# A fused attention and mixture-of-experts kernel: the tile scheduling layer replaced by a recorder with its own semaphores

## Chip, cores, metric

One Trainium2 chip, one NeuronCore. The metric is the device time of one execution in microseconds; the kernel before has a median of 174.42 us over three runs (174.42 to 174.47). Five engines matter: TensorE (PE, its weight loads PEld), VectorE (DVE), ScalarE (ACT), GpSimd (POOL) and SyncE (SP), which here only issues DMAs and waits. Sixteen DMA engines carry all data between memory and SBUF.

## What is computed

Linear attention over 8 batches of 8 heads (576 positions, 64 columns a head), a normalization of each row, and a soft mixture of 8 experts with 4 slots each over all 4608 tokens. All arithmetic is in float32.

```python
kv = np.einsum('bhsd,bhse->bhde', k, v)
out = np.einsum('bhsd,bhde->bhse', q, kv)
x = out / np.sqrt(np.mean(out * out, axis=-1, keepdims=True) + 1e-06) * g_norm   # -> (4608, 512)
logits = x @ phi                                   # 32 slots
d = softmax(logits, over tokens);  slot_input = d.T @ x
slot_out[e] = np.maximum(slot_input[e] @ w1[e], 0.0) @ w2[e]
result = softmax(logits, over slots) @ slot_out
```

## The kernel before, in words

The 4608 tokens are 36 tiles of 128. For each batch the kernel builds the 64x64 products of k and v (class `Kv`, products at L195, L210), places them with phi in a block-diagonal matrix `bd`, and for each token tile multiplies q with it (`products`, L254 and L263), squares, evicts and normalizes. Tiles go in 19 stages of two or one, and six groups of six tiles, each with a running maximum and a partial sum over tokens. After the last group come eight experts (`expert_h` L638, `expert_y` L656), then the mixing of their outputs back to the tokens: `output`, called for two column halves, three token chunks and two parts each, twelve times in all, with products at L701, evictions on ACT (L712) and DVE (L714, the split ones L709 and L710).

All inputs live in one SBUF arena of 160 KB a partition, whose places are written out by hand in tables (`KV_AT`, `Q_AT`, `W_AT`, `OUT_AT`): a place is loaded, read, then overwritten by a later load or by the staged output. Every DMA is issued from SP: `load_row` (L85) and the first load (L123) bring k, v and q; `load_w` (L114) brings the expert weights in eight rows; L718 stores the output in four pieces. There are 24 DMAs. The order of the work is that of the program text: the context manager at L777 takes `manual_schedule`, so the layer orders nothing. What it does is three things. It gives the tiles of each pool (`const`, `wk`, `psA`, `psB`) an address, buffers of a tag taking turns. It works out from the addresses which instruction has to wait for which, and puts semaphore waits and increments on the instructions; for DMAs it has eight semaphores that take turns, and a DMA waits for the one that held its semaphore before. At the end (all its instructions carry L777) SP waits for the DMAs, all engines meet in a barrier, POOL clears the range of semaphores, and all meet again. An earlier barrier at the start belongs to the program's constructor (L769).

The two pools of PSUM have these banks: `psA` two buffers of two banks for `o`, two banks for `kv`, one each for `m` and `s`; `psB` two banks for `y` and three buffers of two banks for `m`.

```python
    const = ctx.enter_context(tc.tile_pool(name="const", bufs=1))
    wk = ctx.enter_context(tc.tile_pool(name="wk", bufs=2))
    ...
    ps = psA.enter_context(tc.tile_pool(name="psA", bufs=1, space=bass.MemoryType.PSUM))
    ...
    ps = ctx.enter_context(tc.tile_pool(name="psB", bufs=3, space=bass.MemoryType.PSUM, reuse_waits="tile"))
```

Of the kernel before, what the change touches and what calls it, by code (L numbers as in the profile page):

```python
# [1 line left out]

# [5 lines left out]

F32 = mybir.dt.float32
BF16 = mybir.dt.bfloat16  # L10
# [4 lines left out]
P = 128  # L15
# [39 lines left out]
SHARED = (5, 11)  # L55
HEAD = 144
SCRATCH = 1024
EPS_RMS = 1e-6
EPS_SUM = 1e-9


def row_length(row):
    return sum(UNIT if part is None else UNIT // 2 for _, _, part in row)


@with_exitstack
def soft_moe_linear_attention(ctx: ExitStack, tc: tile.TileContext, first_in, kv_in, q0_in, q1_in, kv4_in, kv5_in, t3_in, w_in, out):


    nc = tc.nc  # L70

    const = ctx.enter_context(tc.tile_pool(name="const", bufs=1))
    wk = ctx.enter_context(tc.tile_pool(name="wk", bufs=2))
    arena = const.tile([P, HEAD + ARENA], F32, name="arena")
    phi_sb = arena[:, :128].rearrange("p (g w n) -> p g w n", g=2, w=2)
    g2 = arena[:, 128:129]
# [71 lines left out]
    eps = const.tile([P, 1], F32, name="eps")  # L148
    nc.gpsimd.memset(eps, EPS_RMS)
    sel32 = const.tile([P, NS], F32, name="sel32")  # L150
# [20 lines left out]
    run_max = [const.tile([P, 1], F32, name=f"rmax{i}") for i in range(2)]  # L171
    acc = const.tile([P, 129], F32, name="acc")

    psA = ExitStack()
    ps = psA.enter_context(tc.tile_pool(name="psA", bufs=1, space=bass.MemoryType.PSUM))


    class Kv:
# [10 lines left out]
        def products(self, r):  # L189
            g, w = divmod(r, 2)  # L190
            main = kv_main(self.b, g).rearrange("p (r w c n) -> p r w c n", r=2, w=2, c=4)
            for c in range(4):
                for i in range(2):
                    lo = 64 * i
                    nc.tensor.matmul(  # L195
                        self.pkv[lo : lo + 64, w, g],
                        lhsT=main[:, w, 1, c, lo : lo + 64],
                        rhs=main[:, w, 0, c, lo : lo + 64],
                        start=c == 0 and (g == 0 or self.b == 0),
                        stop=False,  # L200
                    )
# [96 lines left out]
    def newton(s):  # L298
        n, ms, r0 = STAGES[s], mss.pop(s), r0s.pop(s)
        r = wk.tile([P, n, H], F32, tag="r", name=f"r{s}", bufs=3)  # L300
        t = wk.tile([P, n * H], F32, tag="r1", name=f"r1{s}")
        nc.vector.scalar_tensor_tensor(out=t, in0=ms, scalar=EPS_RMS, in1=r0, op0=ALU.add, op1=ALU.mult)
        nc.vector.scalar_tensor_tensor(out=t, in0=t, scalar=-0.5, in1=r0, op0=ALU.mult, op1=ALU.mult)
# [120 lines left out]
    first = {b: 9 * (b // 2) + 4 * (b % 2) for b in range(B)}  # L424
# [53 lines left out]
    for g in range(2):  # L478
        kv = Kv(0, "o" if g else "kv", 2 if g else None)
# [10 lines left out]
    for T in range(NT - 2):  # L490
# [3 lines left out]
        o = products(T)  # L494
        s = ends.get(T - 1)
# [36 lines left out]
    s, G = len(STAGES) - 1, len(GROUPS) - 1  # L532
# [51 lines left out]
    last = NE - 1  # L584
# [10 lines left out]
    rs = const.tile([P, 1], F32, name="rs")  # L595
    nc.vector.tensor_scalar_add(rs, acc[:, 128:129], EPS_SUM)
    nc.vector.reciprocal(rs, rs)
    psA.close()


    ps = ctx.enter_context(tc.tile_pool(name="psB", bufs=3, space=bass.MemoryType.PSUM, reuse_waits="tile"))
    W = 2 * GROUPS[0] + 1

    def combine(k):
# [7 lines left out]
        nc.vector.tensor_reduce(out=cs, in_=C, axis=AX.X, op=ALU.add)  # L612
        nc.vector.tensor_scalar_add(cs, cs, EPS_SUM)
        nc.vector.reciprocal(cs, cs)
# [151 lines left out]
def build_program():  # L766
    import concourse.bacc as bacc

    nc = bacc.Bacc("TRN2", target_bir_lowering=False, num_devices=1, dynamic_dma_scratch_size=SCRATCH)  # L769
    shapes = {  # L770
        "first": (P, HEAD + 2304), "kv": (4, P, TOK), "q0": (P, TOK), "q1": (P, 2048),
        "kv4": (P, 2560 + TOK), "kv5": (P, 2 * TOK), "t3": (P, 3 * TOK),
        "w": (1, 2 * NE * P * UNIT),
    }
    args = [nc.dram_tensor(f"in_{n}_dram", s, F32, kind="ExternalInput").ap() for n, s in shapes.items()]
    args.append(nc.dram_tensor("out_0_dram", (1, 4 * NCH * P * 4 * CT * NS), F32, kind="ExternalOutput").ap())
    with tile.TileContext(nc, schedule_with_timeline_sim=True) as tc, tc.manual_schedule():  # L777
        soft_moe_linear_attention(tc, *args)
    return nc


# [56 lines left out]
```

## Time and profile before

| what | value |
|---|---|
| median of 3 runs | 174.42 us (174.42 to 174.47) |
| profiled execution, first to last instruction (its span) | 172.9 us |
| median less span | 1.5 us |
| instructions | 4638 |
| busy: PE, PEld, DVE, ACT, POOL | 150.1, 109.0, 86.3, 89.0, 57.2 us |
| bytes read and written | 61.94 MB and 9.44 MB |
| granted TensorE clock, mean | 0.976 |

The profiled execution has no time of its own beside its span; what the runs' time holds beyond the span is not in the profile. Times in the rows are from the span's start. "PEld" are weight loads, which overlap products. A "q" behind an engine's name means its sequencer: it waits, issues a DMA or handles semaphores, and is not counted as busy. The granted clock is 1.00 in every stretch with products and falls to 0.50 only after the last of them.

### The profile page before, as it was taken

To read this page: it belongs to the slowest core of one execution; us is meant where nothing else is said; L and a number is where in the kernel's file an instruction comes from. 1 tells how busy PE (TensorE), PEld (TensorE's weight loads), DVE (VectorE), ACT (ScalarE), POOL (GpSimd) and SP (SyncE) were. 2 spreads that over 40 slices of the span, in tenths; PEclk is the share of its full clock that TensorE was granted. 3 is DMA by queue.
4 is the path that set the end of the run, shared out by engine and by line. 5 is a ranking of instruction groups with operands and counts; after the bars stand their busy time and mean duration, and the time that the engine had idled before them with its cause. 6 is when DMAs were issued, how large, how long until landed. Compare 5 with 4: busy or idle time off the path is not lost.

```text
span 172.9 us, 4638 instructions
## 1 busy us (share of the span) xinstructions
PE 150.1 (87%) x1975; PEld 109.0 (63%) x1975; DVE 86.3 (50%) x184; ACT 89.0 (51%) x230; POOL 57.2 (33%) x68
## 2 busy tenths in 40 slices
PE   7888897989999899999899989889999989989300
PEld 3457777889688888898796766346665544545000
DVE  1122156383677364763926897625887036228300
ACT  2036486787966888668759863203223035227400
POOL 6000708548356665456582489100000000000000
PEclk9999999999999999999999999999999999999955
DMA  5999999999999998999999998999999999999994
GB/s 188 417 429 426 446 403 449 438 424 471 413 409 443 479 461 359 394 453 402 451 468 428 426 425 368 426 445 400 459 419 428 425 425 403 443 392 401 453 392 199
DMA packets 3476, 71.67 MB, mean 414 GB/s; under 512 B 384, under 2 KB 384, under 8 KB 384
## 3 DMA queue, kind: packets, MB, share of 16 engines
q1 hardware_dynamic: 3456, 71.38, 97.0%
q8 instruction: 15, 0.25, 0.6%
q14 instruction: 5, 0.04, 0.1%
HBM read 61.94 MB, written 9.44 MB: 413 GB/s over the span
## 4 chain that ended last, share of the span: by engine, by line
PE 50%; DMA 23%; ACT 10%; DVE 6%; issue 3%; SPq 2%; DVEq 0%
PE o L263 16%; DMA arena<-in_kv_dram 13%; DMA arena<-in_w_dram 10%; PE kvp_kv L195 8%; PE po L701 5%; PE pY L656 5%; PE pS L412 4%; PE ph L638 2%; PE fill L467 2%; ACT sq L273 2%; PE o L254 2%; ACT arena L712 2%; ACT bd L230 1%; ACT xall L281 1%; SPq L85 1%
## 5 line engine op out<-in xcount | busy, mean ns | idle before, releaser
L263 PE MATMUL o<-bd,arena 128*128 128x192 f32 x256 | 49.3, 336 | 1.7 <-ACT bd L240 1.1
L263 PEld LDWEIGHTS o<-bd,arena 128*128 128x128 f32 x256 | 40.8, 190 | 5.0 <-ACT bd L240 1.6
L286 DVE TENSOR_REDUCE ms<-sq 128x16 f32<-128x1024 f32 (+1 forms) x19 | 22.1, 1162 | 32.2 <-ACT sq L273 32.0
L313 POOL TENSOR_TENSOR xall<-xall,r 128x512 f32<-128x512 f32 x34 | 34.8, 1046 | 0.0
L335 POOL TENSOR_TENSOR part<-part,r 128x512 f32<-128x512 f32 x17 | 17.8, 1050 | 50.4 <-DVE r L304 44.9
L273 ACT ACTIVATE sq<-o 128x512 f32<-128x512 f32 x36 | 21.5, 598 | 11.9 <-PE o L263 11.6
L281 ACT COPY xall<-o 128x512 f32<-128x512 f32 x34 | 20.6, 606 | 0.0
L195 PE MATMUL kvp_kv<-arena 128*64 128x64 f32 x480 | 17.3, 225 | 2.6 <-DMA arena<-in_kv_dram 1.9
L195 PEld LDWEIGHTS kvp_kv<-arena 128*64 128x64 f32 x480 | 15.2, 138 | 6.5 <-DMA arena<-in_kv_dram 2.8
L348 DVE TENSOR_REDUCE logits<-part 128x64 f32<-128x512 f32 (+1 forms) x18 | 17.8, 992 | 0.0
L656 PE MATMUL pY<-arena,xall 128*32 128x256 f32 x256 | 15.0, 380 | 0.2 <-DMA arena<-in_w_dram 0.2
L701 PE MATMUL po<-logits,z 32*128 32x384 f32 x96 | 12.8, 521 | 1.5 <-ACT arena L712 0.9
L638 PE MATMUL ph<-arena,sTe 128*32 128x256 f32 x224 | 12.7, 379 | 0.3 <-DVE sTe L585 0.3
L712 ACT COPY arena<-po 128x768 f32<-128x768 f32 x12 | 9.1, 801 | 7.4 <-PE po L701 7.4
L714 DVE COPY arena<-po 128x768 f32<-128x768 f32 x10 | 9.3, 955 | 7.0 <-PE po L701 7.0
L656 PEld LDWEIGHTS pY<-arena,xall 128*32 128x32 f32 x256 | 8.4, 110 | 6.7 <-issue 1.6
L280 ACT COPY part<-o 128x256 f32<-128x256 f32 x34 | 12.6, 370 | 0.0
L412 PE MATMUL pS<-xall,d 128*32 128x129 f32 x288 | 10.8, 277 | 1.2 <-ACT d L400 1.1
L701 PEld LDWEIGHTS po<-logits,z 32*128 32x128 f32 x96 | 6.1, 183 | 7.1 <-ACT arena L712 4.2
L638 PEld LDWEIGHTS ph<-arena,sTe 128*32 128x32 f32 x224 | 7.2, 110 | 5.3 <-DVE sTe L585 0.7
L412 PEld LDWEIGHTS pS<-xall,d 128*32 128x32 f32 x288 | 7.2, 109 | 4.4 <-issue 3.5
L294 ACT ACTIVATE r<-ms,eps 128x16 f32<-128x16 f32 x17 | 5.2, 308 | 5.9 <-DVE ms L286 5.9
(99 smaller groups left out, 148.3 us busy)
## 6 DMA issues: line engine op xcount, KB each, us to landing
arena<-in_w_dram SPq DMA_DIRECT2D x4, 4096.0 KB, 19.8
arena<-in_w_dram SPq DMA_DIRECT2D x1, 7168.0 KB, 27.6
arena<-in_t_dram SPq DMA_DIRECT2D x1, 6912.0 KB, 36.4
arena<-in_w_dram SPq DMA_DIRECT2D x1, 5120.0 KB, 17.8
arena<-in_kv_dram SPq DMA_DIRECT2D x2, 2304.0 KB, 23.6
arena<-in_kv_dram SPq DMA_DIRECT2D x1, 4608.0 KB, 43.1
out_dram<-arena SPq DMA_DIRECT2D x2, 2304.0 KB, 9.5
arena<-in_kv_dram SPq DMA_DIRECT2D x1, 3584.0 KB, 32.3
```

The source lines that it names most:

```text
L195: nc.tensor.matmul(self.pkv[lo : lo + 64, w, g], lhsT=main[:, w, 1, c, lo : lo + 64], rhs=main[:, w, 0, c, lo : lo + 64], start=c == 0 and ...
L263: nc.tensor.matmul(o[:, r, :192], lhsT=q_main(2 * g + i)[:, r, at : at + P], rhs=bds[i][:, r], start=True, stop=True)
L273: nc.scalar.activation(sqs[s][:, T - starts[s]], o[:, :, 32:160], AF.Square, scale=0.125)
L281: nc.scalar.copy(xts[T % NX][:, :, :128], o[:, :, 32:160])
L286: nc.vector.tensor_reduce(out=mss[s], in_=sqs.pop(s).rearrange("p t j (w d) -> p (t j w) d", w=2), axis=AX.X, op=ALU.add)
L313: nc.gpsimd.tensor_tensor(out=x, in0=x, in1=r[:, i].rearrange("p (j w) -> p j w", w=2).unsqueeze(3).to_broadcast([P, 4, 2, D]), op=ALU.mult,)
L335: engine.tensor_tensor(out=part, in0=part, in1=rs_of[s].unsqueeze(3).to_broadcast([P, STAGES[s], H, NS]), op=ALU.mult)
L348: nc.vector.tensor_reduce(out=L[:, pos(starts[s]) : pos(starts[s]) + STAGES[s]], in_=parts.pop(s).rearrange("p t h n -> p t n h"), axis=AX ...
L412: nc.tensor.matmul(pS[32 * j : 32 * j + 32], lhsT=ds[G][:, i], rhs=x[:, j], start=i == 0, stop=i == GROUPS[G] - 1)
L638: nc.tensor.matmul(ph[32 * j : 32 * j + 32], lhsT=sTe[:, (4 * e + c) * NS : (4 * e + c + 1) * NS], rhs=w_block("w1", e, 4 * c + j), start= ...
L656: nc.tensor.matmul(pY[32 * j : 32 * j + 32, hf, :256], lhsT=hTs[e][:, c], rhs=w_block("w2", u, at + c), start=e == 0 and c < 4, stop=e == ...
L701: nc.tensor.matmul(po[:, 0 if apart else u, : CT * NS].rearrange("p (g x) -> p g x", g=2), lhsT=z[f][lo : lo + 32], rhs=cT[k][lo : lo + 32 ...
```

## The change

The layer goes, and with it its context managers. In its place the kernel file has its own small classes. `Order` stands where the program object stood: each call on an engine (`nc.vector...`) is written down with its operands, `add` works out what it has to wait for, `settle` drops what is already known, and `emit` issues all of it in the same order with semaphores.

```diff
+WORK = {
+    "kvT": (1, 256), "sq": (2, 1024), "part": (3, 512), "ms": (3, 16), "r0": (2, 16), "r": (3, 16), "r1": (2, 16),
+    "top": (1, 128), "diag": (1, 32), "d": (2, 192), "alpha": (2, 1), "cm": (2, 13), "cs": (2, 13),
+}
...
+    def add(self, engine, method, args, kwargs):
...
+        for ap in reads:
+            m = self.memories.get(ap.tensor.name)
+            if m is not None:
+                rows, cols = m.cells(ap)
+                for w in np.unique(m.writer[rows, cols]):
+                    if w >= 0 and (self.ops[w].engine != engine or self.ops[w].dma or engine != "tensor"):
+                        deps.add(int(w))
+                if m.bank:
+                    self.others(deps, m, rows, cols, engine)
+        m = self.memories.get(out.tensor.name) if out is not None else None
+        if m is not None:
+            rows, cols = m.cells(out)
+            for w in np.unique(m.writer[rows, cols]):
+                if w >= 0 and (self.ops[w].engine != engine or self.ops[w].dma):
+                    deps.add(int(w))
+            self.others(deps, m, rows, cols, engine)
...
+    def settle(self, op, deps):
+        known = self.known[op.engine]
+        for d in sorted(deps, reverse=True):
+            w = self.ops[d]
+            key = ("dma", d) if w.dma else w.engine
+            if known.get(key, -1) >= d:
+                continue
+            op.waits.append(w)
+            w.signals = True
+            known[key] = d
+            for k, v in w.known.items():
+                if known.get(k, -1) < v:
+                    known[k] = v
+        op.known = dict(known)
+
+    def emit(self):
+        nc = self.nc
+        counters = {e: nc.alloc_semaphore(f"done_{e}") for e in ENGINES[:4]}
...
+            *before, last = sorted(op.waits, key=lambda w: w.i) or [None]
+            for w in before:
+                engine.wait_ge(w.sem, w.value)
+            inst = getattr(engine, method)(*args, **kwargs)
+            if last is not None:
+                inst.wait_op(last.sem, last.value, "sem-ge")
+            if op.dma:
+                op.sem, op.value = nc.alloc_semaphore(f"dma_{op.i}"), 16
+                sems.append(op.sem)
+                inst.then_inc(op.sem, 16)
+            elif op.signals:
+                counts[op.engine] += 1
+                op.sem, op.value = counters[op.engine], counts[op.engine]
+                inst.then_inc(op.sem, 1)
+        for op in self.ops:
+            if op.dma and not op.signals:
+                nc.sync.wait_ge(op.sem, 16)
+        numbers = sorted(s.num for s in sems)
+        assert numbers == list(range(numbers[0], numbers[-1] + 1))
+        nc.sync.sem_clear(range(numbers[0], numbers[-1] + 1))
...
-    const = ctx.enter_context(tc.tile_pool(name="const", bufs=1))
-    wk = ctx.enter_context(tc.tile_pool(name="wk", bufs=2))
+    const = Const(nc)
+    wk = Pool({tag: [nc.sbuf([P, n], F32, f"{tag}{i}") for i in range(bufs)] for tag, (bufs, n) in WORK.items()})
+    banks = nc.psum(8)
...
-    ps = psA.enter_context(tc.tile_pool(name="psA", bufs=1, space=bass.MemoryType.PSUM))
+    ps = pool(o=(2, 0, 2), kv=(2, 4), m=(1, 6), s=(1, 7))
...
-    ps = ctx.enter_context(tc.tile_pool(name="psB", bufs=3, space=bass.MemoryType.PSUM, reuse_waits="tile"))
+    ps = pool(y=(2, 0), m=(2, 2, 4, 6))
...
-    with tile.TileContext(nc, schedule_with_timeline_sim=True) as tc, tc.manual_schedule():
-        soft_moe_linear_attention(tc, *args)
+    order = Order(nc)
+    soft_moe_linear_attention(order, *args)
+    order.emit()
```

`Memory` keeps for each tensor the last writer and the last reader of every cell: four groups of 32 partitions by single columns in SBUF, by banks of 512 columns in PSUM. In PSUM a reader also waits for readers of the same bank on other engines (`others`). `Pool.tile` gives the buffers of a tag in turn. A DMA has a semaphore of its own. Only an operation that someone waits for increments its engine's semaphore. At the end SP waits for those DMAs that nobody waited for (the four stores) and clears the range of semaphores; the other engines stop after their last instruction. The body of the kernel, its order and its loads and stores are the same text.

## Rows read from the trace of the kernel before

**Rows 1.** The page: the span, and busy time by engine.
```profile
span 172.9 us, 4638 instructions
...
PE 150.1 (87%) x1975; PEld 109.0 (63%) x1975; DVE 86.3 (50%) x184; ACT 89.0 (51%) x230; POOL 57.2 (33%) x68
```

**Rows 2.** The page: busy tenths of the DMA engines in 40 slices; packets, MB, share.
```profile
DMA  5999999999999998999999998999999999999994
...
q8 instruction: 15, 0.25, 0.6%
```

**Rows 3.** Busy by stretch: us, busy (count) by engine; last clock, DMA share, GB/s.
```profile
0.00:1.70 1.70, 0.65 (x2) 0.28 (x3) 0.53 (x2) 0.97 (x1) 0.89 (x8) 1.00 0.00 0
...
20.00:68.00 48.00, 45.27 (x602) 39.44 (x603) 27.34 (x56) 36.17 (x100) 26.73 (x27) 1.00 1.01 432
...
71.00:104.00 33.00, 31.28 (x404) 26.57 (x406) 21.87 (x47) 24.84 (x71) 19.25 (x19) 1.00 1.02 435
...
151.90:153.40 1.50, 1.50 (x29) 0.94 (x32) 0.46 (x1) 0.48 (x1) 0.00 (x0) 1.00 0.78 332
```

**Rows 4.** Timeline of SP: DMA issues, their start and duration in us.
```profile
0.74 0.38 SPq L123 DMA_DIRECT2D arena<-in_first_dram  x1
...
1.64 0.42 SPq L85 DMA_DIRECT2D arena<-in_q_dram  x1
2.11 0.65 SPq L85 DMA_DIRECT2D arena<-in_kv_dram  x1
...
145.43 0.35 SPq L718 DMA_DIRECT2D out_dram<-arena  x1
...
152.53 0.34 SPq L718 DMA_DIRECT2D out_dram<-arena  x1
...
158.18 0.33 SPq L718 DMA_DIRECT2D out_dram<-arena  x1
...
162.28 0.33 SPq L718 DMA_DIRECT2D out_dram<-arena  x1
```

**Rows 5.** The same issues in order: KB each, us from issue to landing.
```profile
arena<-in_q_dram SPq DMA_DIRECT2D x1, 1024.0 KB, 9.9
...
arena<-in_kv_dram SPq DMA_DIRECT2D x1, 1152.0 KB, 13.4
...
out_dram<-arena SPq DMA_DIRECT2D x1, 2304.0 KB, 10.3
...
out_dram<-arena SPq DMA_DIRECT2D x1, 2304.0 KB, 8.7
...
out_dram<-arena SPq DMA_DIRECT2D x1, 1536.0 KB, 6.7
...
out_dram<-arena SPq DMA_DIRECT2D x1, 3072.0 KB, 9.8
```

**Rows 6.** Waits of SP's queue: us in total, times, longest.
```profile
SPq L114 <- PE o L263: 26.8, 2, 21.6
...
SPq L85 <- DMA arena<-in_kv_dram: 9.7, 2, 5.5
SPq L85 <- DMA arena<-in_q_dram: 9.4, 1, 9.4
...
SPq L777 <- DMA out_dram<-arena: 9.2, 2, 7.2
```

**Rows 7.** Instructions of L777 after 172.05 us: ns min/median/max, first and last start.
```profile
L777 SPq EVENT_SEMAPHORE  x1: 28/28/28, 172.1 to 172.1; - x1
...
L777 POOLq EVENT_SEMAPHORE  x4: 17/17/17, 172.2 to 172.8; - x4
...
L777 PEldq EVENT_SEMAPHORE  x2: 51/51/51, 172.4 to 172.9; - x2
...
L777 POOLq EVENT_SEMAPHORE_RANGE_CLEAR  x1: 96/96/96, 172.5 to 172.5; - x1
```

**Rows 8.** DMA packets from 11.6 to 15.4 us, instruction fetches: packets, MB, share.
```profile
q8 instruction: 1, 0.02, 1.5%
```

More of the change, by code (lines that the diff above doesn't have):

```diff
@@ L1 @@
-from contextlib import ExitStack
-import concourse.bass as bass
-import concourse.tile as tile
+import numpy as np
 from concourse import mybir
 from concourse.masks import make_identity
-from concourse._compat import with_exitstack
 F32 = mybir.dt.float32
@@ L57, with __init__, cells @@
 SCRATCH = 1024
+WORK = {
+    "kvT": (1, 256), "sq": (2, 1024), "part": (3, 512), "ms": (3, 16), "r0": (2, 16), "r": (3, 16), "r1": (2, 16),
+    "top": (1, 128), "diag": (1, 32), "d": (2, 192), "alpha": (2, 1), "cm": (2, 13), "cs": (2, 13),
+}
 EPS_RMS = 1e-6
 EPS_SUM = 1e-9
+ENGINES = ("tensor", "vector", "scalar", "gpsimd", "sync")
+class Memory:
+    def __init__(self, tensor, cols, bank=None):
+        self.bank = bank
+        n = -(-cols // (bank or 1))
+        self.pitch = cols
+        self.writer = np.full((4, n), -1, np.int32)
+        self.readers = np.full((len(ENGINES), 4, n), -1, np.int32)
+        self.stores = []
+    def cells(self, ap):
+        (step, rows), *dims = ap.ap
+        first, col = divmod(ap.offset, self.pitch)
+        last = first + (rows - 1) * (step // self.pitch)
+        at = np.array([col])
+        for step, n in dims:
+            if step and n > 1:
+                at = (at[:, None] + step * np.arange(n)).reshape(-1)
+        return slice(first // 32, last // 32 + 1), np.unique(at // (self.bank or 1))
@@ new lines, with __init__, __getattr__, call @@
+class Op:
+    def __init__(self, i, engine, call, dma):
+        self.i, self.engine, self.call, self.dma = i, engine, call, dma
+        self.waits, self.known, self.signals, self.value = [], None, False, 0
+class Engine:
+    def __init__(self, order, name):
+        self.order, self.name = order, name
+    def __getattr__(self, method):
+        def call(*args, **kwargs):
+            self.order.add(self.name, method, args, kwargs)
+        return call
+class Order:
+    def __init__(self, nc):
+        self.nc = nc
+        self.ops, self.memories = [], {}
+        self.known = {e: {} for e in ENGINES}
+        for e in ENGINES:
+            setattr(self, e, Engine(self, e))
+    def sbuf(self, shape, dtype, name):
+        n = int(np.prod(shape[1:]))
+        t = self.nc.alloc_sbuf_tensor(name, [shape[0], n], dtype).ap()
+        self.memories[t.tensor.name] = Memory(t, n)
+        return shaped(t, shape)
+    def psum(self, banks):
+        t = self.nc.alloc_psum_tensor("psum", [P, banks * 512], F32).ap()
+        self.memories[t.tensor.name] = Memory(t, banks * 512, bank=512)
+        return t.rearrange("p (b n) -> p b n", n=512)
+    def add(self, engine, method, args, kwargs):
+        op = Op(len(self.ops), engine, (method, args, kwargs), method == "dma_start")
+        self.ops.append(op)
+        named = dict(kwargs)
+        rest = list(args)
+        out = named.pop("out") if "out" in named else rest.pop(0) if rest and hasattr(rest[0], "tensor") else None
+        reads = [x for x in rest + list(named.values()) if hasattr(x, "tensor")]
+        if out is not None and method == "matmul" and not kwargs["start"]:
+            reads.append(out)
+        deps = set()
+        for ap in reads:
[14 more added lines that the diff above has]
+            self.others(deps, m, rows, cols, engine)
+            for i, where in m.stores:
+                if overlap((rows, cols), where):
+                    deps.add(i)
+        self.settle(op, deps)
+        for ap in reads:
+            mr = self.memories.get(ap.tensor.name)
+            if mr is not None:
+                rows, cols = mr.cells(ap)
+                if op.dma:
+                    mr.stores.append((op.i, (rows, cols)))
+                else:
+                    mr.readers[ENGINES.index(engine)][rows, cols] = op.i
+        if m is not None:
+            m.writer[m.cells(out)] = op.i
+    def others(self, deps, m, rows, cols, engine):
+        for e, name in enumerate(ENGINES):
+            if name != engine:
+                r = int(m.readers[e][rows, cols].max())
+                if r >= 0:
+                    deps.add(r)
+    def settle(self, op, deps):
[15 more added lines that the diff above has]
+        counters = {e: nc.alloc_semaphore(f"done_{e}") for e in ENGINES[:4]}
+        sems = list(counters.values())
+        counts = dict.fromkeys(counters, 0)
+        for op in self.ops:
+            method, args, kwargs = op.call
+            engine = getattr(nc, op.engine)
+            *before, last = sorted(op.waits, key=lambda w: w.i) or [None]
[4 more added lines that the diff above has]
+                inst.wait_op(last.sem, last.value, "sem-ge")
+            if op.dma:
+                op.sem, op.value = nc.alloc_semaphore(f"dma_{op.i}"), 16
[5 more added lines that the diff above has]
+                inst.then_inc(op.sem, 1)
+        for op in self.ops:
+            if op.dma and not op.signals:
[3 more added lines that the diff above has]
+        nc.sync.sem_clear(range(numbers[0], numbers[-1] + 1))
@@ new lines, in overlap, with shaped, flat_banks, __init__ @@
+def overlap(a, b):
+    (ra, ca), (rb, cb) = a, b
+    return ra.start < rb.stop and rb.start < ra.stop and len(np.intersect1d(ca, cb, assume_unique=True)) > 0
+def shaped(t, shape):
+    dims = " ".join(f"d{i}" for i in range(len(shape) - 1))
+    return t.rearrange(f"p ({dims}) -> p {dims}", **{f"d{i}": n for i, n in enumerate(shape[1:])})
+def flat_banks(banks, at, n):
+    return banks[:, at : at + n].rearrange("p b n -> p (b n)")
+class Pool:
+    def __init__(self, slots):
+        self.slots = slots
+        self.turn = dict.fromkeys(slots, 0)
+    def tile(self, shape, dtype, tag, name=None, bufs=None):
+        slots = self.slots[tag]
+        t = slots[self.turn[tag] % len(slots)]
+        self.turn[tag] += 1
+        return shaped(t[:, : int(np.prod(shape[1:]))], shape)
@@ L62, in row_length, with __init__, tile, soft_moe_linear_attention @@
+class Const:
+    def __init__(self, nc):
+        self.nc = nc
+    def tile(self, shape, dtype, name):
+        return self.nc.sbuf(shape, dtype, name)
 def row_length(row):
     return sum(UNIT if part is None else UNIT // 2 for _, _, part in row)
-@with_exitstack
-def soft_moe_linear_attention(ctx: ExitStack, tc: tile.TileContext, first_in, kv_in, q0_in, q1_in, kv4_in, kv5_in, t3_in, w_in, out):
-    nc = tc.nc
-    const = ctx.enter_context(tc.tile_pool(name="const", bufs=1))
-    wk = ctx.enter_context(tc.tile_pool(name="wk", bufs=2))
+def soft_moe_linear_attention(nc, first_in, kv_in, q0_in, q1_in, kv4_in, kv5_in, t3_in, w_in, out):
+    const = Const(nc)
+    wk = Pool({tag: [nc.sbuf([P, n], F32, f"{tag}{i}") for i in range(bufs)] for tag, (bufs, n) in WORK.items()})
+    banks = nc.psum(8)
@@ L172, in soft_moe_linear_attention, with pool @@
     acc = const.tile([P, 129], F32, name="acc")
-    psA = ExitStack()
-    ps = psA.enter_context(tc.tile_pool(name="psA", bufs=1, space=bass.MemoryType.PSUM))
+    def pool(**tags):
+        return Pool({tag: [flat_banks(banks, b, n) for b in at] for tag, (n, *at) in tags.items()})
+    ps = pool(o=(2, 0, 2), kv=(2, 4), m=(1, 6), s=(1, 7))
     class Kv:
@@ L597, in soft_moe_linear_attention @@
     nc.vector.reciprocal(rs, rs)
-    psA.close()
-    ps = ctx.enter_context(tc.tile_pool(name="psB", bufs=3, space=bass.MemoryType.PSUM, reuse_waits="tile"))
+    ps = pool(y=(2, 0), m=(2, 2, 4, 6))
     W = 2 * GROUPS[0] + 1
```

## The prediction

> **What bounds the kernel now.** I read the page's totals first. TensorE looks like the limit: 87% of a span of 172.9 us [rows 1]. Next the DMA slices: all sixteen DMA engines are at 90% or more from the second slice to the last but one [rows 2]. Two resources look full, so the question is which one makes the other wait. Busy time by stretch tells: nothing moves until 1.7 us (the first load is issued at 0.74, so about 1.0 us passes from issue to first byte), then the load stretches 20 to 68 and 71 to 104 us run at 432 and 435 GB/s with a share of 1.01 and 1.02 [rows 3, 4]. A queue at one steady rate never lacks work. The one hollow to be seen, 151.9 to 153.4 us, still has a share of 0.78 [rows 3].
>
> For the loads those stretches settle it. For the four output stores, the last in the queue, I set each issue on SP beside the landing of the DMA ahead of it. They are issued at 145.43, 152.53, 158.18 and 162.28 and land 10.3, 8.7, 6.7 and 9.8 us later, that is at 155.7, 161.2, 164.9 and 172.1 [rows 4, 5]. Each follower is issued 3.2, 3.0 and 2.6 us before its predecessor has landed. So on the DMA engine that finishes last there is always work, and the last landing, 172.1, is set by bytes over rate, not by TensorE. What SP does after the last issue is wait: 9.2 us for stores [rows 6].
>
> Last, the end. SP's wait on the fourth store starts again at 172.1 (28 ns). After it stand a gathering on POOL (four semaphore steps from 172.2 to 172.8), a clear of the semaphore range on POOL (96 ns at 172.5) and a second release of all engines, the last of them TensorE's 51 ns step at 172.9 [rows 7]. From landing (172.08) to the end of the span is 0.82 us in which no data moves.
>
> **The change, part by part.** (1) The end. It removes the two barriers and puts four waits and one range clear on SP. What is left after the last landing: one wait of 28 ns, 0.05 us from one SP instruction to the next (SP's issue at 1.64 takes 0.42, the next starts at 2.11 [rows 4]), one clear. The trace has that clear only on POOL, 96 ns [rows 7]; on SP it costs between nothing and, if it were as slow as all that stands there now, 0.82 us. I take 96 ns, the nearest row. New end 0.17 us, gain 0.82 - 0.17 = 0.65 us, with bounds 0 and 0.79 (the wait alone left). Nothing covers this stretch, so all of it reaches the span.
>
> (2) One semaphore per DMA in place of eight that take turns. SP now waits, before it reuses a semaphore, for the DMA that held it, 9.7 us for kv and 9.4 for q loads [rows 6]. Those waits go, but what is late next is the data hazard behind them: a load overwrites a place in the arena, and SP then waits for TensorE's last read (26.8 us on L263 [rows 6]). And were a load issued earlier, it would only queue behind loads in flight. I cost it at nothing; the cover is the full DMA queue.
>
> (3) The waits on the five engines. The new rule counts exact columns and drops waits that another implies, so some waits fall away; on the other side an instruction with several waits now spends one semaphore instruction for each. Below: TensorE gains a little. Above: 51 ns for each extra one on TensorE [rows 7]; one more for each of the 24 half tiles of output is 1.2 us. I take zero on the path, because the fourth store may come late by 2.6 less the 1.0 us of start-up, 1.6 us, before the last DMA engine runs dry [rows 3 to 5]. If that cover were used up, each further microsecond would be one of span.
>
> (4) The buffers. Work buffers keep their number (part 3, sq 2, o 2 x 2 banks, m 1, then m 3 x 2 banks), so who waits for which buffer stays. But they are now allotted ahead of the arena, 18.4 KB a partition by the list WORK, and the arena moves by that. Cost: nothing, or the rival below.
>
> Nothing is moved on a queue: SP issues the same 24 DMAs in the same order, and the other engines keep their order. Start: the barrier before the first issue comes from the program's constructor (L769), not from the layer removed.
>
> **Sum.** Span 172.9 - 0.65 = 172.25 us. The runs' median, 174.42, lies 1.52 us above this span; I leave that as it is: 173.77 us. Its own range: 0.82 us gone at most, plus 0.2 either way for the DMA stream, gives 173.4; the clear three times as dear and the stream 0.2 later gives about 174.05.
>
> **Rivals.** A change under 0.2% (0.35 us) is what a measurement here cannot tell from none; so the end alone, 0.65, would show.
>
> A. *Slower: an instruction fetch hits the last DMA engine.* Instruction blocks come over the same sixteen DMA engines: 15 packets, 0.6% [rows 2]. From 11.6 to 15.4 us there is one such packet with 1.5% of that stretch's DMA time [rows 8], and the 1152 KB load issued at 2.11 lands at 15.5, while the one ahead (issued 1.64) landed at 11.5: 4.0 us, where 1.18 MB at 432 GB/s take 2.7 [rows 3 to 5]. So one fetch on an unlucky engine costs up to 1.2 us, and never comes back because the queue is never empty. The change shifts every instruction after the first dropped wait, hence the fetches. If one more falls on the last engine: 173.77 + 1.2 = 174.97. It decides as soon as that engine gets one fetch more than now; against it, the stream shortens by few instructions out of 4638, so the number of blocks stays near 15. One fetch fewer there would give 172.6 by the same price. The Trainium skill, page "Runtime: NRT & Kernel Launch", section "Instruction fetch mechanics", holds that crossing a 16 KiB block is mostly hidden. By it this rival would not exist and the sum would stay at 173.77; the landing above disagrees for a kernel whose DMA queue is full.
>
> B. *Faster still: the moved arena suits the DMA engines.* Every transfer has its SBUF side in the arena, and all its addresses shift. If the rate rose everywhere from the 432 GB/s of one stretch to the 435 of the other [rows 3], 0.7% of 170 us or 1.2 us would go as well: 172.6. Against it: the last store, out of the arena, runs at 3.15 MB in 7.2 us, 437 GB/s, no slower than the loads into it [rows 5]; the place seems not to matter. The Trainium skill, page "DMA: Bandwidth & Descriptors", section "How a descriptor splits into AXI transactions", has a rule for this: a read that starts off a 256-byte boundary fetches unused bytes from the boundary below. By it only the stores could gain (they alone read the arena), an estimate of at most 8 beats for each of 32 rows a DMA engine, some 0.3 us; no row here shows it.
>
> C. *No change.* The end is short in the kernel, but what is timed closes on something else in the 1.52 us around the span, or a small loss in the DMA stream eats most of 0.65: 174.4. For it: no row shows what that 1.52 us is. Against it: four engines would be done 10 us earlier and SP alone would close.
>
> **How the numbers follow.** Forecast 0.70, A 0.11, B with the lucky half of A 0.07, C 0.12. The likeliest gives 173.77. The range takes in the forecast (173.4 to 174.05) and C (174.4), and leaves out A and B, 0.18: 173.2 to 174.5, the lower end a little under the forecast's own because an earlier finish of four engines may also shorten what follows. Faster by over 0.2%: forecast less 0.01 of its upper edge, and B, 0.76. Slower: A, 0.11. Within: the rest, 0.13.
>
> **What would show it.** Right: the fourth store still issued near 162.3 and landed near 172.1, SP the only engine with instructions after that, ending within 0.2 us; slices of DMA unchanged. Wrong by A: the same issues, but the last landing about a microsecond later, with a load whose interval is 1.2 us too long. Wrong by B: stretches at 435 GB/s or more and the last landing before 171. Wrong in (3): fourth store issued after 163.9. Wrong in (1): a long range clear, or a barrier on all engines after it.

## The result and the profile after

The changed kernel takes 172.52 us (median of four runs, 172.44 to 172.67) against 174.44 for the kernel before beside it: ratio 0.989, 95% interval 0.9876 to 0.9904. That is 1.92 us, three times the 0.65 forecast in the sum and below the range (173.2 to 174.5). The direction was right, the size was not.

The page of the changed kernel, to be laid beside [rows 1, 2]: span, busy time by engine, DMA slices, instruction fetches.

```profile
span 171.2 us, 4497 instructions
...
PE 149.1 (87%) x1975; PEld 108.1 (63%) x1975; DVE 86.0 (50%) x184; ACT 88.9 (52%) x230; POOL 57.2 (33%) x68
...
DMA  5999999999999999999999999998999999999995
...
q8 instruction: 15, 0.25, 0.5%
```

141 instructions are gone and the engines do the same work in the same time; the DMA engines are as full as before, and there are 15 instruction fetches again. In the new file every instruction is issued from `emit`, so all lines below read L204 (the instruction itself), L203 (a wait ahead of it), L217 and L220 (the end), and all PSUM tiles are called `psum`.

Busy time by stretch, the stretches of [rows 3], last column GB/s:

```profile
20.00:68.00 48.00, 45.23 (x604) 39.37 (x605) 27.24 (x56) 36.27 (x101) 26.70 (x27) 1.00 1.02 437
71.00:104.00 33.00, 31.48 (x422) 26.80 (x420) 21.73 (x49) 25.23 (x72) 19.86 (x20) 1.00 1.02 439
```

437 and 439 GB/s stand where 432 and 435 stood. This is the first surprise: nothing in the change was meant to make the DMA engines faster. SP's timeline shows what came of it, the four stores of [rows 4]:

```profile
144.24 0.35 SPq L204 DMA_DIRECT2D out_dram<-arena  x1
...
151.57 0.34 SPq L204 DMA_DIRECT2D out_dram<-arena  x1
...
157.04 0.33 SPq L204 DMA_DIRECT2D out_dram<-arena  x1
...
161.19 0.33 SPq L204 DMA_DIRECT2D out_dram<-arena  x1
```

and their landings, KB and us, as in [rows 5]:

```profile
out_dram<-arena SPq DMA_DIRECT2D x1, 2304.0 KB, 10.5
...
out_dram<-arena SPq DMA_DIRECT2D x1, 2304.0 KB, 8.6
...
out_dram<-arena SPq DMA_DIRECT2D x1, 1536.0 KB, 6.8
...
out_dram<-arena SPq DMA_DIRECT2D x1, 3072.0 KB, 9.9
```

Each store is issued about 1.1 us earlier and takes as long as before; the last lands at 171.1 instead of 172.1. The weights that the experts wait for came that much earlier, so TensorE did too: the products that wait for the last of them start at 134.7 instead of 135.8 us.

The end, instructions of L217 and L220 (ns min/median/max, first and last start), against [rows 7]:

```profile
L217 SPq EVENT_SEMAPHORE  x2: 17/22/28, 163.8 to 171.1; - x2
...
L220 SPq EVENT_SEMAPHORE_RANGE_CLEAR  x1: 78/78/78, 171.1 to 171.1; - x1
```

After the last landing there is one wait and a clear of 78 ns, and the span ends at 171.2. Waits of SP's queue, against [rows 6]:

```profile
SPq L204 <- PE psum L204: 116.8, 10, 23.1
```

No wait of a load for a load is left in that view; the time is now put down to TensorE's last read of the place, as forecast.

One more thing stands in the results: each run has its time and the span of the same execution. The kernel before has 172.6 to 172.7 us of span in nine later runs and 1.80 us around it (medians); the execution profiled at first, 172.9, was a long one, so its difference to the median of other executions, 1.52, was not what lies around. The changed kernel has 171.2 and 1.34. Of 1.9 us, then, about 1.4 are in the span and 0.5 around it.

### The profile page after: what moved, and what is told of

Read it like the earlier page. It is cut to its first block, busy times and chain, and to the rows that moved or that the text cites. A ratio compares the mean times of both kernels' runs of the same rounds, so it can differ in the third digit from the quotient of the medians.

```text
span 171.2 us, 4497 instructions
## 1 busy us (share of the span) xinstructions
PE 149.1 (87%) x1975; PEld 108.1 (63%) x1975; DVE 86.0 (50%) x184; ACT 88.9 (52%) x230; POOL 57.2 (33%) x68
## 4 chain that ended last, share of the span: by engine, by line
PE 47%; DMA 26%; ACT 12%; DVE 5%; SPq 2%; issue 1%
PE psum L204 47%; DMA arena<-in_kv_dram 13%; DMA arena<-in_w_dram 13%; ACT bd L204 3%; ACT sq L204 3%; ACT xall L204 2%; SPq L204 2%; DVE logits L204 1%; ACT arena L204 1%; DVE ms L204 1%; ACT part L204 1%; ACT d L204 1%; ACT r L204 1%; DVE r L204 0%; DVE d L204 0%
## 5 line engine op out<-in xcount | busy, mean ns | idle before, releaser
L204 PE MATMUL psum<-bd,arena 128*128 128x192 f32 (+1 forms) x320 | 56.1, 335 | 1.9 <-ACT bd L204 1.5
L204 PEld LDWEIGHTS psum<-bd,arena 128*128 128x128 f32 (+1 forms) x320 | 45.4, 179 | 7.1 <-ACT bd L204 2.8
L204 DVE TENSOR_REDUCE ms<-sq 128x16 f32<-128x1024 f32 (+1 forms) x19 | 22.1, 1162 | 32.6 <-ACT sq L204 32.3
L204 POOL TENSOR_TENSOR xall<-xall,r 128x512 f32<-128x512 f32 x34 | 34.8, 1044 | 0.0
L204 POOL TENSOR_TENSOR part<-part,r 128x512 f32<-128x512 f32 x17 | 17.8, 1049 | 49.7 <-DVE r L204 49.7
L204 ACT ACTIVATE sq<-psum 128x512 f32<-128x512 f32 x36 | 21.5, 598 | 12.6 <-PE psum L204 12.4
L204 PE MATMUL psum<-arena 128*64 128x64 f32 (+1 forms) x640 | 21.7, 226 | 3.3 <-DMA arena<-in_kv_dram 2.2
L204 PEld LDWEIGHTS psum<-arena 128*64 128x64 f32 (+1 forms) x640 | 19.0, 137 | 7.9 <-DMA arena<-in_kv_dram 3.5
L204 ACT COPY xall<-psum 128x512 f32<-128x512 f32 x34 | 20.6, 606 | 0.0
L204 ACT COPY part<-psum 128x256 f32<-128x256 f32 (+1 forms) x38 | 13.6, 359 | 9.9 <-DVE part L204 8.8
L204 DVE TENSOR_REDUCE logits<-part 128x64 f32<-128x512 f32 (+1 forms) x18 | 17.8, 991 | 0.0
L204 PE MATMUL psum<-arena,xall 128*32 128x256 f32 x256 | 15.0, 380 | 0.4 <-DMA arena<-in_w_dram 0.2
L204 DVE COPY arena<-psum 128x768 f32<-128x768 f32 (+1 forms) x12 | 10.4, 889 | 8.4 <-PE psum L204 8.4
L204 ACT COPY arena<-psum 128x768 f32<-128x768 f32 (+1 forms) x14 | 10.1, 755 | 8.3 <-PE psum L204 8.3
L204 PE MATMUL psum<-logits,part 32*128 32x384 f32 x96 | 12.8, 521 | 1.5 <-ACT arena L204 0.9
L204 PE MATMUL psum<-arena,sq 128*32 128x256 f32 x224 | 12.7, 379 | 0.2 <-DVE sq L204 0.2
L204 PEld LDWEIGHTS psum<-arena,xall 128*32 128x32 f32 x256 | 8.0, 110 | 7.3 <-DMA arena<-in_w_dram 1.8
L204 PE MATMUL psum<-xall,d 128*32 128x129 f32 x288 | 10.8, 278 | 0.9 <-ACT d L204 0.9
L204 ACT COPY bd<-psum 64x128 f32<-64x128 f32 (+1 forms) x32 | 9.9, 309 | 1.6 <-PE psum L204 1.4
L204 PEld LDWEIGHTS psum<-logits,part 32*128 32x128 f32 x96 | 6.1, 183 | 7.1 <-ACT arena L204 4.2
L204 PEld LDWEIGHTS psum<-arena,sq 128*32 128x32 f32 x224 | 7.2, 110 | 5.2 <-DVE sq L204 0.6
L204 PEld LDWEIGHTS psum<-xall,d 128*32 128x32 f32 x288 | 7.0, 109 | 4.1 <-ACT d L204 2.2
```

The lines of the kernel that those rows point to most:

```text
L204: inst = getattr(engine, method)(*args, **kwargs)
```

## The experiments

Three theories. *P*: the moved arena (its places are at 192 bytes past a multiple of 256 in the kernel before, by its list of allocations, which no trace shows, and at a multiple in the new one; the runs themselves show only what a shift does) sets the pace of the DMA engines. *W*: the shorter list of waits did it; the trace has 160 semaphore instructions before and 31 after. *E*: the end costs more than it shows. Medians; the ratio is to the kernel before on the same chip.

| kernel | us | ratio, 95% | span | around |
|---|---|---|---|---|
| e1 before, arena +64 B | 173.71 | 0.9961 (0.9949 to 0.9974) | 171.9 | 1.80 |
| e2 changed, arena +192 B | 173.24 | 0.9934 (0.9921 to 0.9946) | 171.9 | 1.32 |
| e4 changed, arena +128 B | 173.12 | 0.9927 (0.9915 to 0.9940) | 171.8 | 1.34 |
| e11 changed, arena +32 B | 173.50 | 0.9944 (0.9932 to 0.9957) | 172.2 | 1.30 |
| e12 changed, arena +256 B | 172.70 | 0.9900 (0.9884 to 0.9915) | 171.4 | 1.34 |
| e5 changed, staged output +192 B | 172.65 | 0.9895 (0.9882 to 0.9909) | 171.3 | 1.32 |
| e6 changed, loads +192 B | 173.37 | 0.9934 (0.9922 to 0.9947) | 172.0 | 1.31 |
| e3 changed, long end | 173.69 | 0.9965 (0.9951 to 0.9979) | 171.9 | 1.79 |
| e7 changed, POOL held | 173.07 | 0.9919 (0.9905 to 0.9932) | 171.4 | 1.71 |
| e8 changed, TensorE held | 172.83 | 0.9905 (0.9890 to 0.9920) | 171.4 | 1.48 |
| e9 changed, ScalarE held | 172.62 | 0.9890 (0.9873 to 0.9908) | 171.3 | 1.30 |
| e10 changed, VectorE held | 172.85 | 0.9898 (0.9880 to 0.9915) | 171.6 | 1.31 |

**The place of the arena.** e1 is the kernel before with two unused tiles, one ahead of the arena and one behind, so that the later tensors keep their place against 256 bytes:

```diff
+    const.tile([P, 16], F32, name="ahead")
     arena = const.tile([P, HEAD + ARENA], F32, name="arena")
+    const.tile([P, 48], F32, name="behind")
```

> The kernel before, with the arena alone moved up by 64 bytes in each partition (192 unused bytes behind it keep every later tensor where it was against 256 bytes), so that its places start where those of the changed kernel start against 256 bytes. Theory P (the place of the arena against 256 bytes set the pace of the DMA engines): the last store lands about 1.0 us earlier, near 171.1 instead of 172.1 us, and the time falls from 174.4 to about 173.4 us (ratio 0.994). Theory W (the shorter list of waits and semaphore steps, or compute that ran ahead, gave the 1.0 us): nothing moves here, 174.4 us, last landing 172.1.

Measured 173.71, 0.70 us less, with every wait of the old layer still there. Busy by stretch (both stretches), then the last store on SP's timeline (the store's line is L720 there), then its KB and us to landing:

```profile
20.00:68.00 48.00, 45.64 (x605) 39.81 (x606) 27.34 (x56) 36.24 (x101) 26.82 (x28) 1.00 1.02 436
71.00:104.00 33.00, 31.36 (x416) 26.67 (x416) 21.81 (x49) 25.11 (x71) 19.82 (x20) 1.00 1.01 434
```
```profile
161.33 0.33 SPq L720 DMA_DIRECT2D out_dram<-arena  x1
```
```profile
out_dram<-arena SPq DMA_DIRECT2D x1, 3072.0 KB, 9.7
```

436 GB/s and a last landing at 171.0: in this profiled execution the whole 1.1 us, in the spans of five runs 0.7. P holds, W falls. The pace must be read from the first stretch: over all traces it is 435 to 437 GB/s there with the loads at a multiple of 256 and 431 or 432 off it. The second stretch does not separate the two (432 to 439 against 432 to 435; here 434, under the 435 before). The last landing does: 171.0 to 171.3 us against 171.8 to 172.1. e2 is the reverse, 48 columns ahead of the arena and 16 behind it in the changed kernel:

> The changed kernel with the arena alone moved up by 192 bytes (64 behind it), back to where it was before against 256 bytes. Theory P: the last landing goes back from 171.1 to about 172.1 us and the time rises from 172.5 to about 173.5 us, the short end and whatever else came with it being kept. Theory W: 172.5 us, no change.

Measured 173.24, 0.72 us more, and the same stretch is back at the old pace:

```profile
20.00:68.00 48.00, 44.89 (x606) 38.98 (x603) 27.20 (x56) 36.07 (x100) 26.54 (x27) 1.00 1.01 431
```

The waits are priced by e1 beside e3 (below): both have the long end and places at a multiple of 256, one with the old waits (160 semaphore instructions), the other with the new ones (43). They take 173.71 and 173.69 us with a span of 171.9 each, so 117 fewer semaphore instructions are worth nothing here. e2 agrees: its span, 171.9, is that of the kernel before (172.6) less the 0.65 of the end. Two more sizes, 32 columns on each side and 8 ahead with 56 behind:

> The changed kernel with the arena alone moved up by 128 bytes (128 behind it): its places then start at half of 256 bytes. Theory P with a step of 256 bytes: slower, by up to the 1.0 us of the other shift (173.0 to 173.5 us). With a step of 128 or 64 bytes: 172.5 us as it was. Theory W: 172.5 us.

> The changed kernel with the arena alone moved up by 32 bytes (224 behind it), so that its places are 32 bytes past a multiple of 256. If any place off a multiple of 256 costs alike, it is like the shifts by 128 and 192 bytes (173.1 and 173.2 us). If places off 64 bytes cost more than those off 256 alone: clearly above 173.3 us. If the cost grows with the distance from the boundary: between 172.5 and 173.0 us.

173.12 and 173.50. The step is not 128 bytes, and the cost does not grow with the distance: 32 bytes is the dearest of the three. The control, 64 columns ahead:

> Control: the changed kernel with the arena and all later tensors moved up by 256 bytes, so that nothing changes against a multiple of 256. If the place against 256 bytes is what counts: 172.5 us. If a shift as such, whatever its size, costs: about 173.2 us like the others.

172.70; its interval covers the changed kernel's ratio, so the step is 256 bytes. Its stretch runs at the fast pace:

```profile
20.00:68.00 48.00, 45.21 (x604) 39.34 (x605) 27.25 (x56) 36.19 (x101) 26.79 (x28) 1.00 1.02 436
```

**Loads or stores.** e5 moves the staged output alone; e6 moves the arena by 192 bytes and the staged output by 64 more:

```diff
+    def staged(at, n):
+        return arena[:, HEAD + at * KB + 48 : HEAD + at * KB + 48 + n]
...
-        st = place(at, 4 * CT * NS).rearrange("p (a n) -> p a n", a=4)
+        st = staged(at, 4 * CT * NS).rearrange("p (a n) -> p a n", a=4)
...
-                    out[:, lo * P : (lo + m) * P].rearrange("o (p n) -> (o p) n", p=P), place(OUT_AT[row[0]], m)
+                    out[:, lo * P : (lo + m) * P].rearrange("o (p n) -> (o p) n", p=P), staged(OUT_AT[row[0]], m)
```

> The changed kernel with only the staged output moved up by 192 bytes in the arena: the four stores read from places 192 bytes past a multiple of 256, all loads still write to multiples of 256. The shift of the whole arena cost 0.72 us. Theory R (the reading side alone counts, as the rule of the Trainium skill's page 'DMA: Bandwidth & Descriptors' on a read that starts off a 256-byte boundary has it): all of the 0.72 us would come from the stores, 173.2 us. Theory S (each row that starts off the boundary costs the same, read or written): the stores are 9.44 of 71.38 MB and 512 of 3072 rows, so 0.1 us, 172.6 us. Theory L (only writes into SBUF count): 172.5 us.

> The changed kernel with the arena moved up by 192 bytes and the staged output by 64 more, so that only the loads land off a multiple of 256 and the stores read from multiples of 256. Theory R (reads alone): 172.5 us, no change. Theory S (every row alike): five sixths of 0.72, 173.1 us. Theory L (writes into SBUF alone): 173.2 us.

Stores off the boundary: 172.65, 0.13 us more. Loads off the boundary: 173.37, 0.85 us more. The load stretch of e5, then of e6:

```profile
20.00:68.00 48.00, 45.24 (x604) 39.37 (x605) 27.25 (x56) 36.29 (x101) 26.64 (x27) 1.00 1.02 436
```
```profile
20.00:68.00 48.00, 44.83 (x601) 38.95 (x602) 27.20 (x56) 35.85 (x100) 26.55 (x27) 1.00 1.01 432
```

Theory R (reads alone) falls: writes into SBUF carry the cost. Whether the stores pay their share too (S) or nothing (L) the 0.13 us cannot settle, since the runs of one kernel spread over as much; for the same reason e6's 0.85 is not more than the 0.72 of e2, which moved both. The packets of the 3072 KB store speak for S: of its 128 rows of 24576 bytes, 110 take exactly 912 ns in the changed kernel and 111 in e6, but 60 in e5 and 58 in the kernel before, where most of the others take longer.

**The end.** e3 gives the changed kernel the old end:

```diff
-        nc.sync.sem_clear(range(numbers[0], numbers[-1] + 1))
+        nc.all_engine_barrier()
+        nc.gpsimd.sem_clear(range(numbers[0], numbers[-1] + 1))
+        nc.all_engine_barrier()
```

> The changed kernel, with SP's range clear replaced by a barrier of all engines, a range clear on POOL and a second barrier, as at the end of the kernel before. If the end is worth what the trace of before shows: the span grows by 0.65 us and the time goes from 172.5 to about 173.2 us. If the four engines that finish early also shorten what lies around the span (it shrank from 1.5 to 1.3 us), 173.4 us. If the end is worth nothing outside the profile: 172.5 us. The last landing stays at 171.1 in each case.

Measured 173.69, 1.17 us more, above each of the cases. POOL's last steps, those of the second barrier:

```profile
L222 POOLq EVENT_SEMAPHORE  x2: 17/17/17, 171.6 to 171.6; - x2
```

The last landing is at 171.0 and the span ends at 171.8; around it stand 1.79 us again. I had expected the 0.48 us around the span to be 0.2, from the wrong 1.52. To see whose it is, four kernels hold one engine each to the end (here POOL):

```diff
+        held = nc.alloc_semaphore("held")
+        sems.append(held)
+        nc.gpsimd.wait_ge(self.ops[-1].sem, 16).then_inc(held, 1)
+        nc.sync.wait_ge(held, 1)
         numbers = sorted(s.num for s in sems)
```

> The changed kernel with POOL kept until the end: it waits for the last store's semaphore too and then lets SP clear the range. What lies around the span was 1.80 us with the long end and 1.33 with the short one. If that 0.48 us is a closing sequence of POOL that ran while SP still waited, the rest is back at about 1.8 and the time near 173.1 us (0.1 us of it the extra step on SP). If it belongs to another engine or needs all of them: 1.33 around the span and 172.6 us.

> The same with TensorE kept until the end in place of POOL. If the 0.48 us is a closing sequence of TensorE: about 1.8 us around the span, time near 173.1 us. If not: 1.33 and 172.6 us.

> The changed kernel with ScalarE alone kept until the end: it waits for the last store's semaphore too and then lets SP clear the range. If the 0.48 us around the span that the short end gave is a closing sequence of ScalarE: about 1.8 us around the span, time near 173.1 us. If not: 1.33 and 172.6 us.

> The same with VectorE kept until the end. If the 0.48 us is a closing sequence of VectorE: about 1.8 us around the span, time near 173.1 us. If not: 1.33 and 172.6 us.

Around the span: 1.71 us with POOL held, 1.48 with TensorE, 1.30 and 1.31 with ScalarE and VectorE, 1.34 with SP alone. In e7 POOL's last step and SP's clear stand like this:

```profile
L220 POOLq EVENT_SEMAPHORE  x1: 17/17/17, 171.0 to 171.0; - x1
```
```profile
L224 SPq EVENT_SEMAPHORE_RANGE_CLEAR  x1: 81/81/81, 171.2 to 171.2; - x1
```

POOL is done 0.2 us before SP and still sets what comes after. So from POOL's last instruction to the end of the run there are some 1.9 us (1.71 + 0.2), from TensorE's about 1.7 (1.48 + 0.2), from SP's 1.3, and ScalarE and VectorE stay below 1.5 (1.3 + 0.2). The kernels with the long end agree: POOL's last step is done 0.09 us before the end of their span (the kernel before, e1 and e3), and 1.8 + 0.09 is 1.9 again. So POOL alone accounts for the 0.48; that more follows TensorE than SP, too, was not among the cases. What POOL does in those 1.9 us no row shows; "closing" is only a name for it. e10's time of 172.85 is above 172.6, but by its span (171.6), not by what lies around it; why its span was longer stays open.

## Why the prediction was wrong, step by step

The two causes cross in the four cells of this table:

| | long end | short end |
|---|---|---|
| places 192 bytes past a multiple of 256 | 174.41 (before) | 173.24 (e2) |
| places at a multiple of 256 | 173.71 (e1), 173.69 (e3) | 172.52 (changed) |

The place is worth 0.70 and 0.72 us, the end 1.17 and 1.17 to 1.19; together they make the 1.9.

**What bounds the kernel**: right, with a slip that changes nothing (the DMA row is a mean of the sixteen engines, and two of its slices inside stand at 8). The DMA queue decides; the stores are issued with the one ahead still in flight, and a faster stream moves all of them by 1.1 us in the trace.

**Part 1, the end**: mechanism right, term mis-sized. In the span it gave what was forecast (0.82 us down to a wait and a clear of 78 ns; 96 was taken). The step that failed is "I leave that as it is": what lies around the span is 1.80 us with the long end and 1.33 with the short one, because POOL's own closing, 0.6 us longer than SP's, now runs long before (POOL is done at 108.1 us). The prediction named this in the range alone ("an earlier finish of four engines") and gave it hardly 0.2. It also took 1.52 us for the surroundings by setting one execution's span against other executions' median; as the sum only takes 0.65 off the median, that did not move it. The upper edge of its own range is added wrongly: a clear three times as dear and 0.2 us of stream give 174.16, not 174.05.

**Parts 2 and 3, semaphores and waits**: right, nothing on the path (e1 beside e3).

**Part 4, the buffers**: the step that failed is "Cost: nothing, or the rival below". Rival B happened, at 0.7 us where it was priced at 1.2, and had 0.07 together with another case. The price was taken from the difference between two stretches of one kernel, whose places are the same, so it measured nothing of the place; that its order of size was right is luck, and so is its 172.6 us beside the 172.52 measured, since it had 1.2 us for the place and nothing for the surroundings where the runs show 0.7 and 0.5. Its evidence against was no evidence: it set the last store beside the loads, and in the kernel before both are off the boundary. A comparison of two things that share the suspected fault cannot clear it. The store was a poor witness besides: between the last two landings it takes 7.2 us on the boundary as well (163.8 to 171.1 in the changed kernel). The rule of the Trainium skill, page "DMA: Bandwidth & Descriptors", section "How a descriptor splits into AXI transactions", had the right boundary of 256 bytes, which e4 and e12 bear out; its text is about reads, and taken as that it gave 0.3 us from the stores, where e6 shows that rows written off the boundary cost most.

**Rival A**: the delay is real, its price is not. In the changed kernel the 1152 KB load lands 4.0 us after the one ahead (1.64 + 9.9 against 2.11 + 13.5), as in [rows 4, 5]. In e12, the same kernel 256 bytes further up, the fetch starts only after that load has landed (14.9 us), and the load needs 1.4 us less. The changed kernel, then e12:

```profile
arena<-in_kv_dram SPq DMA_DIRECT2D x1, 1152.0 KB, 13.5
```
```profile
arena<-in_kv_dram SPq DMA_DIRECT2D x1, 1152.0 KB, 12.0
```

All fourteen traces go this way: with the fetch at 13.1 to 13.9 us the load lands at 15.3 to 15.9, with the fetch at 14.9 us or later at 14.0 to 14.3. But e12's last store lands at 171.05 us, the changed kernel's at 171.06, and e4 (load at 14.2) and e2 (15.8) both end with a landing at 171.8. So the delay does come back, and "never comes back because the queue is never empty" was wrong for this fetch, and the late landing no evidence of a cost in the time. A fetch more on the last engine near the end was not seen in any run.

**Rival C**: refuted, the end reaches the time and more than that.

## What to carry to other kernels

Where the DMA queue is full from end to end, look up where each buffer starts: here starting the arena at a multiple of 256 bytes was worth 0.7 us (0.4%) for 256 unused bytes a partition, without any other change. Finish on SP and let POOL (by some 0.6 us here) and TensorE (by some 0.3) go early; a last barrier costs its own 0.65 us and another 0.5 that no profile row of the kernel shows. Take what lies around a span from runs that give both numbers, not from one profile and another run's median.

## What was not expected

A row of 18432 bytes takes exactly 686 ns in 489 of 512 packets of the changed kernel, and in 203 of 512 of the kernel before, where most of the others take 2 to 10 ns longer. The loss is one for each row, and from 18432 bytes on about the same on long rows and short ones (rows of 9216 bytes show hardly any). Of the 128 loaded rows of 28672 bytes, 126 take 1062 ns in the changed kernel; in the kernel before 66 take 1065 and 25 take 1072. Of those of 55296 bytes, 123 take 2041 ns; before, 68 take 2044 and 25 take 2051. The times of all packets, summed and divided by the sixteen engines, come to 168.9 us in the kernel before and 168.1 in e1, which is the size of the gain. The packets also follow the order of the shifts: that by 32 bytes (173.50) costs more than those by 192 and 128 (173.24, 173.12), and at 32 bytes most of the 55296-byte rows take 2045 or 2052 ns, a nanosecond more than at 192. Why the distance matters in this order is open.
